# Numerators of an attention unit in groups of 7, 7 and 6 tiles, with a new order of all work

## The chip, the core and the metric

The kernel runs on one core of a Trainium2 chip. The core has a matrix engine (TensorE, PE in the profile, with its weight loads as PEld), a vector engine (VectorE, DVE), a scalar engine (ScalarE, ACT), a general engine (GpSimd, POOL) and a sync engine (SP) that here only issues transfers. The engines run side by side, each in the order of its own instructions, and wait for each other through semaphores. The matrix engine writes to PSUM, which has 8 banks of 2 KB in each of 128 partitions. The metric is the device time of one execution in microseconds (us), lower is better.

## The reference

Eight batches with eight heads of 576 tokens and 64 values each go through a linear attention with the feature map exp(p - max|p|), exp(-p - max|p|), where p is a projection to 128 features. The result, 4608 tokens of 512 values, goes through a feed-forward layer that takes the greatest of three products.

```
def phi(x):
    proj = x @ w_phi                                  # 64 -> 128
    proj = proj - max(|proj|, axis=-1)
    return concat([exp(proj), exp(-proj)], axis=-1)   # 256 features
kv  = phi(k)^T v ;  z = sum over tokens of phi(k)
num = phi(q) kv  ;  den = phi(q) z + 1e-6
x   = (num / den)       # heads side by side: (B*S, H*D)
h   = max(x @ w1, x @ w2, x @ w3)                     # 512 -> 768
out = h @ w_out                                       # 768 -> 512
```

## The kernel before, in words

The attention runs in 16 units of four heads (half a batch). The four heads are two pairs `pr`, each of two heads `ab`. The 576 tokens of a pair are kept in nine tiles of 64 tokens for each of its two heads, so a unit has 18 tiles of 128 rows; features stand on 128 partitions.

A unit goes through these pieces, each of them a `Node` of some kind. `L` and `Lv` load q, k and v in fp32 over SP's queue; `C` casts q and k to bf16 on POOL. From unit 4 on, `T` is one transposing transfer on SP's queue (line 495) that makes `qkT`, 18 tiles of 128x128; in the first four units TensorE transposes. `G` (line 518) projects q and k for up to four tiles into two banks; `r` (line 537) reduces them to their greatest absolute values on DVE, and `ek` (line 531) takes the exponentials of k on ACT. `R`, `mT` and `V` turn the maxima of q and write them as one row into `qkT` by a small transfer (line 553). `M` (line 597) projects q once more with the features on partitions, and `eq` (line 610) takes its exponentials, in five parts, one for each pair and head and one for the rest. `E`, `va` and `vd` scale v by the maxima of k. `K` (line 626) makes kv and z for both heads `ab` in two banks, and `kv` copies them out.

`N` (line 644) makes the numerators with the denominators beside them: a tile is 128 tokens by 65 values, two accumulating products. Before the change a group is one pair and one head `ab`: five tiles, the fifth of them from the rest. It needs the kv of its own `ab`, two `eq` of its part and the two of the rest. `x` (lines 650 and 651) takes the reciprocals of the five denominators and multiplies 128x320 values by them into `x_sb`, which is kept as pair, tile, head, value, so that a write steps over the other head. A unit has four such groups, each with a bank of its own. `X` (line 674) then carries all of `x_sb` to `xT` by one transposing transfer on SP's queue (the first two units use TensorE).

The feed-forward layer works on `xT` in nine chunks of 512 tokens, one for each batch and a ninth for the last 64 tokens of all batches. In a chunk there are twelve `up` and `up2` products of four matmuls each (line 697), whose results DVE and ACT take out, and four output tiles: four matmuls (line 725) and six (line 730), a copy `osb` (line 738) and a `store` (line 745). A tile of chunks 0 to 7 is stored by two transfers of 64 rows, one of chunk 8 by one transfer of 128 rows. The weights enter as differences, `wd` (line 768).

The order of all this comes from a planner and is written out: `PLAN` (lines 95 to 231) is a list of words such as `301S2@59.7`, which is node number 301, engine SP, buffer 2, due time 59.7. A letter T, D, A, G or S tells the engine (PE, DVE, ACT, POOL, SP). The kernel records the instructions in the list's order, engine by engine; nothing in the program waits for a due time. The due times also tell `fill` where TensorE's order has a gap in which it puts products on constant data (`idler`, line 827), nearly all before 28 us. The number of a node is its place in the order of creation, so the numbers differ between the two lists.

Three places of the list before, with the transposing transfer of a unit and the first projection that uses it:

```
301S2@59.7  ... 307T013201@67.2      unit 4
691S1@117.9 ... 712T107610@127.4     unit 10
756S0@146.2 ... 767T016110@154.6     unit 11
```

The functions that the change touches follow; the profile's line numbers stand beside them.

Of the kernel before, what the change touches and what calls it, by code (L numbers as in the profile page):

```python
# [19 lines left out]
P = 128  # L20
# [15 lines left out]
KPE = 1.04  # L36
GROUPS = [(0, 4), (4, 4), (9, 4), (13, 4), (8, 2)]
# [58 lines left out]
2D1@0.7 4A@0.7 85G1@0.7 10S1@0.7 3D@1.1 6S0@1.1 86G@1.5 8S@1.5 13S@2.0 0G@2.3 15S3@2.4 1076G@2.9 5D@3.4 159G0@3.6 12D2@3.9  # L96
158G@4.5 1079G@5.2 7A@5.7 1G@6.0 16T5@6.4 1077G@6.5 17D2@7.2 9A@7.4 27T103510@7.9 361S0@8.2 22T27@8.2 30D@8.4 31D@9.0 14A@9.1
26D@9.6 29A@9.7 20T4@9.9 18T6@10.0 21D@10.3 24A@10.3 25D@10.5 28A@10.8 19D@11.1 23A@11.3 42T54@11.4 46D@11.8 32T76@11.9 45D@12.1
43A@12.2 36D@12.4 44A@12.6 47A0@12.8 37T34@13.0 35D@13.0 39A@13.5 40D@13.6 93T7@13.8 33A@13.9 94D0@14.2 87D1@14.5 34A@14.5
115T012701@14.6 88S@14.7 58T30@14.7 118D@15.0 117A@15.0 61T5@15.3 41D@15.3 59A@15.5 64T2@15.8 48D1@15.9 38A@16.0 89T6@16.3  # L100
63A@16.5 67T4@16.9 60A@17.0 90D@17.1 91T0@17.2 66A@17.5 119D@17.7 51A@17.9 92D@18.1 62A@18.2 53G@18.3 1086T3@18.3 68A@18.6
65A@18.9 105T15@19.0 1087D1@19.0 69A@19.4 54G@19.4 55T2@19.5 228G1@19.7 108D@20.2 57A@20.3 227G@20.5 116A@20.7 95T14@20.9
56A@21.0 100T63@21.1 364G2@21.3 103D@21.6 102A@21.6 96A@22.1 98D@22.2 110T60@22.3 52G@22.4 97A@22.7 109D@22.8 166T2@23.1
162T1@23.2 113D@23.4 107A@23.5 11G@23.5 1078G@23.7 114D@24.0 106A@24.1 137T61@24.1 49G@24.5 101A@24.6 163D2@24.6 164T7@24.6
139A@25.0 167D@25.2 165D@25.5 1088T2@25.6 138A@25.6 50G@25.6 1090T1@26.0 124A1@26.1 1089D@26.3 112A@26.3 127G0@26.5 140T5@26.5
70T167@26.7 125G@26.7 1091A@26.8 99D@27.4 111A@27.7 126G@27.9 1096T2@27.9 72D@28.2 141A@28.2 71A@28.5 104D@28.5 142A@28.7
120A@29.3 173T106010@29.3 1097A@29.6 122G@29.6 183T51@29.6 1094T7@29.9 176D@29.9 174A@30.1 187D@30.5 186D@31.1 184A@31.2
73T31@31.3 75T4@31.6 175A@31.7 160D3@31.7 74D1@31.8 128T5@31.9 161S@31.9 1082G@32.1 1095A@32.1 134T6@32.4 362S1@32.4 76D0@32.4
185A@32.6 297S0@32.8 79T2@32.8 135A@33.1 178T47@33.2 80D0@33.4 131T3@33.5 136A@33.7 426S0@33.8 177D@34.0 77T2@34.2 121G@34.2
133A@34.3 1098T6@34.5 181D@34.6 129A@34.8 229D2@35.2 132A@35.3 78D1@35.3 123G@35.3 1080G@35.6 168T01@35.8 182D@35.9 1099A@36.0  # L110
143T032@36.1 171D@36.5 130A@36.5 179A@37.0 172D@37.1 188T60@37.3 231T5@37.4 144A@37.5 192D@37.7 145A@37.8 170A@38.1 191D@38.1
148T20@38.2 232D0@38.4 1092T4@38.5 196A1@38.5 190A@38.7 198G1@38.9 169A@39.0 149D1@39.0 189A@39.5 152T6@39.8 1093A@40.1
83T0@40.1 153D1@40.4 235T5@40.4 180A@40.6 146T4@40.7 197G@41.0 236D@41.0 84A@41.0 81T6@41.1 147D0@41.3 193T5@41.5 150T7@41.5
199A@41.7 233T1@41.8 82A@41.8 194D1@42.0 151D0@42.2 195S@42.3 154T4@42.4 234D@42.8 242T012601@42.8 230S@43.0 365G@43.1 155A@43.1
# [165 lines left out]
def kernel(  # L280
# [133 lines left out]
    def attention(u):  # L414
# [214 lines left out]
        for ab in range(2):  # L629
# [229 lines left out]
```

## Time and profile before

| what | value |
|---|---|
| median of 3 runs | 289.76 us (289.59 to 290.92) |
| the profiled execution | 290.44 us, its span 288.7 us |
| busy: PE, DVE, ACT, POOL | 279.6, 204.9, 197.8, 121.8 us |
| transfers | 51.45 MB, mean 178 GB/s |
| transposing transfers on SP | 12 of `qkT`, 14 of `xT` |

The span is the time from the first to the last instruction that the profiler saw on this core; the time of the execution has 1.7 us around it. A row of a view by line gives the place in the kernel, the engine, the operation with its tiles, the count, then the busy time in us and the mean of one in ns, and after the second bar the idle time of that engine just before, with what ended it. In a row of waits stand the engine and line that waited, what for, and then total, times and longest in us. [...]

### The profile page before, as it was taken

How to read it: one execution, taken by the hardware profiler on the slowest of the kernel's cores; microseconds unless marked ns; L12 is line 12 of the kernel's file. 1: busy time of each engine (PE TensorE's matmuls, PEld its weight loads, DVE VectorE, ACT ScalarE, POOL GpSimd, SP SyncE). 2: the span in 40 equal slices, each digit the busy share in tenths (PEclk: the TensorE clock that was granted, in tenths of full speed). 3: DMA queues.
4: the chain of work that ended last, by engine and by line, in shares of the span. 5: the costliest groups of instructions: out<-in, count | busy, mean ns of one | idle time of the engine just before them, and what ended most of it. 6: DMA issues, size and time to landing. Idle time of an engine off the chain costs nothing.

```text
span 288.7 us, 8634 instructions
## 1 busy us (share of the span) xinstructions
PE 279.6 (97%) x3587; PEld 155.0 (54%) x3587; DVE 204.9 (71%) x431; ACT 197.8 (69%) x456; POOL 121.8 (42%) x104
## 2 busy tenths in 40 slices
PE   8999999998999999999998999999999999999994
PEld 3466675465565655556455466565544654444452
DVE  3978888897999787967788778897976362156210
ACT  2799898998989998886896978977664501330021
POOL 8048969949517159564552634062162000000000
PEclk9999999999999999999999999999999999999999
DMA  7999979999989999999999988869400037610064
GB/s 184 275 251 209 236 280 205 283 309 210 178 208 257 254 262 238 246 213 272 209 231 226 257 177 201 210 136 143 82 4 0 2 75 144 139 30 0 6 157 130
DMA packets 68193, 51.45 MB, mean 178 GB/s; under 512 B 48762, under 2 KB 52922, under 8 KB 68154
## 3 DMA queue, kind: packets, MB, share of 16 engines
q1 hardware_dynamic: 63759, 45.55, 66.6%
q0 software_dynamic: 4000, 4.92, 9.9%
q8 instruction: 28, 0.46, 0.7%
q10 hardware_dynamic: 395, 0.43, 0.4%
q14 instruction: 11, 0.09, 0.1%
HBM read 34.64 MB, written 9.44 MB: 153 GB/s over the span
## 4 chain that ended last, share of the span: by engine, by line
PE 75%; DMA 15%; ACT 5%; DVE 2%; SPq 1%; issue 1%; ACTq 0%
PE ups L697 29%; PE ops L730 13%; DMA qkT<-qk_bf 9%; PE ops L725 9%; PE psn L644 5%; PE psq L518 5%; PE kvps L626 4%; PE psm L597 4%; DMA k_raw<-in_k_dram 2%; ACT Eq L610 2%; DMA xT<-x_sb 2%; PE pm L796 2%; ACT Ek L531 2%; DMA qkT<-mT 1%; DVE mqp L537 1%; PE idler L827 1%
## 5 line engine op out<-in xcount | busy, mean ns | idle before, releaser
L697 PE MATMUL ups<-xT,w_bf 128*128 128x512 bf16 x432 | 102.0, 379 | 0.2
L610 ACT ACTIVATE Eq<-psm 128x512 bf16<-128x512 f32 (+1 forms) x160 | 80.4, 575 | 18.6 <-PE psm L597 17.6
L531 ACT ACTIVATE Ek<-psk 128x512 bf16<-128x512 f32 (+1 forms) x160 | 81.8, 574 | 9.8 <-PE psk L518 7.3
L572 POOL TENSOR_TENSOR vab<-v_raw,em 128x1152 bf16<-128x1152 f32 (+1 forms) x35 | 67.2, 1929 | 50.2 <-ACT em L568 44.5
L697 PEld LDWEIGHTS <-w_bf 128*128 128x128 bf16 x432 | 40.2, 98 | 44.7 <-issue 0.4
L537 DVE TENSOR_REDUCE mqp<-psq 128x4 bf16<-128x512 f32 (+1 forms) x80 | 49.0, 633 | 10.8 <-PE psk L518 7.8
L537 DVE TENSOR_REDUCE mk<-psk 128x4 f32<-128x512 f32 (+1 forms) x80 | 49.4, 630 | 4.6 <-PE psk L518 2.7
L730 PE MATMUL ops<-wout_bf,hT 128*128 128x512 bf16 (+1 forms) x222 | 51.5, 373 | 0.0
L703 DVE TENSOR_TENSOR hT<-hT,ups 128x512 bf16<-128x512 bf16 x54 | 35.8, 682 | 11.9 <-PE ups L697 10.0
L738 ACT COPY osb<-ops 128x512 f32<-128x512 f32 (+1 forms) x21 | 12.2, 586 | 30.8 <-PE ops L730 13.4
L651 DVE TENSOR_TENSOR x_sb<-psn,rden 128x320 bf16<-128x320 f32 x64 | 31.5, 492 | 2.2
L644 PEld LDWEIGHTS <-Eq 128*128 128x128 bf16 x640 | 26.8, 97 | 11.4 <-DVE x_sb L651 0.4
L730 PEld LDWEIGHTS <-hT 128*128 128x128 bf16 x222 | 20.8, 98 | 21.2 <-DVE hT L703 0.2
L705 ACT ACTIVATE hT<-ups 128x512 bf16<-128x512 f32 x33 | 19.6, 607 | 18.1 <-PE ups L697 16.9
L644 PE MATMUL psn<-kv_sb,Eq 128*128 128x65 bf16 x640 | 29.3, 194 | 0.3 <-DVE x_sb L651 0.3
L738 DVE COPY osb<-ops 128x512 f32<-128x512 f32 (+1 forms) x16 | 10.7, 670 | 25.4 <-PE ops L730 12.7
L518 PE MATMUL psq<-w,qkT 64*128 64x128 bf16 x288 | 24.1, 217 | 2.7 <-DMA qkT<-qk_bf 2.6
L518 PEld LDWEIGHTS <-qkT 64*128 64x128 bf16 x576 | 16.5, 94 | 16.2 <-issue 9.6
L725 PE MATMUL ops<-xT 128*128 128x512 bf16 x96 | 24.5, 379 | 0.0
L518 PE MATMUL psk<-w,qkT 64*128 64x128 bf16 x288 | 24.1, 217 | 0.0
L466 POOL CAST qk_bf<-k_raw 128x1152 bf16<-128x1152 f32 x12 | 13.7, 1146 | 22.7 <-DMA k_raw<-in_k_dram 22.7
L597 PE MATMUL psm<-qkT,wphi_m 128*128 128x512 bf16 (+1 forms) x70 | 21.8, 358 | 0.3 <-DMA qkT<-mT 0.3
(71 smaller groups left out, 245.2 us busy)
## 6 DMA issues: line engine op xcount, KB each, us to landing
v_raw<-in_v_dram SPq DMA_DIRECT2D x16, 576.0 KB, 5.5
out_dram<-osb SPq DMA_DIRECT2D x65, 128.0 KB, 2.5
q_raw<-in_q_dram SPq DMA_DIRECT2D x12, 576.0 KB, 7.0
k_raw<-in_k_dram SPq DMA_DIRECT2D x12, 576.0 KB, 6.0
w_bf<-in_moe_w_dram POOLq DMA_DIRECT2D x3, 768.0 KB, 14.7
qk_bf<-in_q_dram POOLq DMA_DIRECT2D x3, 288.0 KB, 12.6
qk_bf<-in_k_dram POOLq DMA_DIRECT2D x3, 288.0 KB, 11.9
wout_bf<-in_moe_w_out_dram POOLq DMA_DIRECT2D x1, 768.0 KB, 20.9
```

The costliest lines, as they stand in the source:

```text
L518: nc.tensor.matmul(ps()[:, i, :], lhsT=cols[r, :], rhs=w2[r, c, :], start=True, stop=True)
L531: nc.scalar.activation(Ek[s]()[:, tiles_of(t0, n), :], of(1), EXP, scale=1.0 - 2.0 * s)
L537: nc.vector.tensor_reduce((mq, mk)[c]()[:, tiles_of(t0, n)], of(c), AXX, ALU.max, apply_absolute_value=True)
L572: (nc.vector if n_.eng == "DVE" else nc.gpsimd).tensor_tensor(vab()[:, g, t0:t1, 0:D], vb()[:, t0:t1, :], em()[:, g, t0:t1].unsqueeze(2).t ...
L597: nc.tensor.matmul(psm()[:, 0:w], lhsT=wphi_m, rhs=rhs, start=True, stop=True)
L610: nc.scalar.activation(Eqb()[s][:, cols], psm()[:, 0:w], EXP, scale=1.0 - 2.0 * s)
L644: nc.tensor.matmul(psn()[:, c, :], lhsT=Eqb()[g][:, t0:t0 + P], rhs=kv()[:, pr, ab, g, :], start=(g == 0), stop=(g == 1))
L651: nc.vector.tensor_tensor(x_sb()[:, pr, :, ab, :], psn()[:, :, 0:D], rden().to_broadcast([P, 5, D]), ALU.mult)
L697: nc.tensor.matmul(ups(), lhsT=w_bf[i + 1][:, ct, j * P:(j + 1) * P], rhs=tokens_of(ct), start=(ct == 0), stop=(ct == CT - 1))
L703: nc.vector.tensor_tensor(hT()[:, j, :], hT()[:, j, :], ups(), ALU.max)
L725: nc.tensor.matmul(ops_()[:, 0:width], lhsT=tile_of(ct, tt), rhs=line_w[c_i > MOVE][:, ct, cols], start=(ct == 0), stop=False)
L730: nc.tensor.matmul(ops_()[:, 0:width], lhsT=hT()[:, j, tt * P:(tt + 1) * P], rhs=wout_bf[:, j, cols], start=False, stop=(j == JT - 1))
```

## The change

The twenty tiles of a unit are numbered in one row: pair (0 or 1), then tile (0 to 4), then head `ab`. They are cut into groups of 7, 7 and 6. `x_sb` is kept as twenty tiles of 64 values, so that the values of a group lie side by side; the addresses of a value are the same as before. A group waits for the kv of both `ab`, for the `eq` of each part that its tiles touch, and for the two of the rest if it has a tile of it: the middle group waits for all ten. The reciprocals are 128x7 or 128x6, the products 128x448 or 128x384. The costs given to the planner for `N` and `x` are now by the tile.

With 32 nodes fewer (1442 for 1474) the whole list is new, planned with transposing transfers that take longer. The instructions of each engine stand in another order from start to end, and some pieces are on another engine: five output copies from ACT to DVE (ACT 21 to 16), seven `vd` from POOL to ACT (POOL 11 to 4), four `mT` from DVE to ACT, two of the six `wd` from POOL to DVE, and two of the first evacuations of `up` from DVE to ACT. There are 38 idlers for 43. SP issues as many loads, stores, T and X as before. The last output tile of the list is one of chunk 7, with two store transfers on SP; before it is one of chunk 8, with one on ACT. The three places of above, and the first `up` product of chunk 1 with the projection groups ahead of it, are in the new list:

```
293S2@58.1  ... 294T112100@66.4      unit 4
671S1@117.3 ... 692T006411@130.5     unit 10
734S0@147.1 ... 740T006711@155.8     unit 11
404T167@74.5 430T003111@75.9 389T2@76.1 435T50@76.6 1120T3@77.6
```

The core of the diff:

```
+NGROUPS = ((0, 7), (7, 14), (14, 20))
...
-        x_sb = buf("x_sb", 2, [P, 2, 5, 2, D], BF16)
+        x_sb = buf("x_sb", 2, [P, 20, D], BF16)
...
-        for pr in range(2):
-            for ab in range(2):
-                psn = bank("psn", [P, 5, W])
...
-                rden = buf("rden", 2, [P, 5, 1], FP32)
...
-                    nc.vector.reciprocal(rden(), psn()[:, :, D:W])
-                    nc.vector.tensor_tensor(x_sb()[:, pr, :, ab, :], psn()[:, :, 0:D], rden().to_broadcast([P, 5, D]),
-                                            ALU.mult)
-                first_eq = 4 * pr + 2 * ab
-                a = nd("N", {"PE": 0.32}, nmm, [n_kvs[ab]] + eqs[first_eq:first_eq + 2] + eqs[8:], [Eqb, kv, psn, x_sb])
-                divs[pr].append(nd("x", {"DVE": 0.62}, div, [a], [psn, x_sb, rden], locks=[psn]))
+        for n0, n1 in NGROUPS:
+            n, heads = n1 - n0, sorted({(i // 10, i % 2) for i in range(n0, n1)})
+            psn = bank("psn", [P, n, W])
+
+            def nmm(n0=n0, n1=n1, psn=psn):
+                for i in range(n0, n1):
+                    pr, c, ab = i // 10, i % 10 // 2, i % 2
+                    t0 = (8 * pr + 4 * ab + c if c < 4 else MT + pr) * P + (D if c == 4 and ab else 0)
+                    for g in range(2):
+                        nc.tensor.matmul(psn()[:, i - n0, :], lhsT=Eqb()[g][:, t0:t0 + P], rhs=kv()[:, pr, ab, g, :],
+                                         start=(g == 0), stop=(g == 1))
+
+            rden = buf("rden", 2, [P, 7, 1], FP32)
+
+            def div(n0=n0, n1=n1, n=n, psn=psn, rden=rden):
+                nc.vector.reciprocal(rden()[:, 0:n, :], psn()[:, :, D:W])
+                nc.vector.tensor_tensor(x_sb()[:, n0:n1, :], psn()[:, :, 0:D], rden()[:, 0:n, :].to_broadcast([P, n, D]), ALU.mult)
+            need = [e for pr, ab in heads for e in eqs[4 * pr + 2 * ab:4 * pr + 2 * ab + 2]]
+            if any(i % 10 // 2 == 4 for i in range(n0, n1)):
+                need += eqs[8:]
+            a = nd("N", {"PE": 0.0628 * n}, nmm, n_kvs + need, [Eqb, kv, psn, x_sb])
+            a = nd("x", {"DVE": 0.307 + 0.0666 * n}, div, [a], [psn, x_sb, rden], locks=[psn])
...
-            done.append(nd("X", {"SP": 1.5}, xdma, divs[0] + divs[1], [x_sb], pipe=1.9, hold=0.5, lat=1.5))
+            done.append(nd("X", {"SP": 1.5}, xdma, divs[0] + divs[1][1:], [x_sb], pipe=1.9, hold=0.5, lat=1.5))
```

More of the change, by code (lines that the diff above doesn't have):

```diff
@@ L100 @@
[L100 to L108, printed above, removed]
@@ new lines, in attention @@
+        for n0, n1 in NGROUPS:
[17 more added lines that the diff above has]
+            a = nd("x", {"DVE": 0.307 + 0.0666 * n}, div, [a], [psn, x_sb, rden], locks=[psn])
+            for j in range(2):
+                if any(i // 10 == j for i in range(n0, n1)):
+                    divs[j].append(a)
@@ L663, in tx @@
                     for c in range(5):
-                        nc.tensor.transpose(pxT()[:, c, :], x_sb()[:, pr, c, :, :].rearrange("p a d -> p (a d)"), ident)
+                        nc.tensor.transpose(pxT()[:, c, :], x_sb()[:, 10 * pr + 2 * c:10 * pr + 2 * c + 2, :].rearrange("p a d -> p (a d)"), ident)
                 def cx(n_, pr=pr, pxT=pxT):
@@ L675, in xdma @@
                     out=xT[:, b, ct0:ct0 + 2, :].rearrange("p q (t c) -> p (q t) c", c=P),
-                    in_=x_sb().rearrange("p q t a d -> p (q t a d)"))
-            done.append(nd("X", {"SP": 1.5}, xdma, divs[0] + divs[1], [x_sb], pipe=1.9, hold=0.5, lat=1.5))
+                    in_=x_sb().rearrange("p t d -> p (t d)"))
+            done.append(nd("X", {"SP": 1.5}, xdma, divs[0] + divs[1][1:], [x_sb], pipe=1.9, hold=0.5, lat=1.5))
         un["done"] = done
```

266 lines of the change are left out of this document (133 added, 133 removed).

## The prediction

> **What bounds the kernel now.** I read the page first, for the engine that is always busy and for the stretches where it is not, then the same by stage, then the waits of that engine, and last the chain.
>
> ```profile
> span 288.7 us, 8634 instructions
> PE 279.6 (97%) x3587; PEld 155.0 (54%) x3587; DVE 204.9 (71%) x431; ACT 197.8 (69%) x456; POOL 121.8 (42%) x104
> PE   8999999998999999999998999999999999999994
> PEclk9999999999999999999999999999999999999999
> ```
>
> TensorE is busy 279.6 of 288.7 us with a granted clock of nine tenths or more in all 40 slices. So the end moves only by what TensorE has to do, by where it stands idle, and by what follows its last product.
>
> ```profile
> 60.00:80.00 20.00, 18.94 (x329) 11.07 (x328) 16.90 (x38) 18.63 (x44) 12.95 (x11) 1.00 0.99 209
> 100.00:120.00 20.00, 19.67 (x301) 10.98 (x301) 17.24 (x38) 17.58 (x46) 15.36 (x11) 1.00 0.98 256
> 120.00:140.00 20.00, 19.57 (x296) 11.56 (x289) 15.40 (x36) 16.24 (x40) 7.47 (x5) 1.00 1.09 225
> 140.00:160.00 20.00, 18.79 (x249) 10.53 (x247) 16.23 (x33) 16.22 (x40) 10.46 (x8) 1.00 1.05 242
> 160.00:180.00 20.00, 20.00 (x311) 11.41 (x309) 14.95 (x33) 17.02 (x41) 9.49 (x8) 1.00 0.94 205
> ```
>
> The columns after the length are the busy time of PE, PEld, DVE, ACT and POOL, then clock, DMA share and GB/s. Beyond 60 us TensorE loses 1.06, 0.33, 0.43 and 1.21 us in four of these stages, 3.0 us together; in the fifth it loses nothing. Its waits for transfers over the whole run (total, times, longest):
>
> ```profile
> PE psq L518 <- DMA qkT<-qk_bf: 2.6, 3, 1.1
> PE psm L597 <- DMA qkT<-mT: 0.3, 1, 0.3
> PEld L518 <- DMA xT<-x_sb: 0.4, 1, 0.4
> ```
>
> They make 3.3 us, about what those stages lose, and each is for a transfer that SP issued. The chain of waits shows which (start, length from issue to landing):
>
> ```profile
> 58.29 9.42 DMA qkT<-qk_bf
> 104.52 4.02 DMA qkT<-mT
> 120.97 7.83 DMA qkT<-qk_bf
> 133.96 6.33 DMA xT<-x_sb
> 148.71 8.81 DMA qkT<-qk_bf
> ```
>
> By order on SP the three long ones are the transposing transfers T of units 4, 10 and 11. The list of before gave them, from issue to first projection, 7.5 us (`301S2@59.7` to `307T013201@67.2`), 9.5 (unit 10) and 8.4 (unit 11). They took 9.42, 7.83 and 8.81; unit 10's was issued 3.07 us after its due time. They landed at 67.71, 128.80 and 157.52, which is 0.5, 1.4 and 2.9 us behind the due time of their first use (67.2, 127.4, 154.6). So the lists can be read as an order with known spacing, and before lost its time against its own at these transfers. I take no duration from a list.
>
> **The change, part by part.**
>
> ```profile
> L651 DVE TENSOR_TENSOR x_sb<-psn,rden 128x320 bf16<-128x320 f32 x64 | 31.5, 492 | 2.2
> L644 PE MATMUL psn<-kv_sb,Eq 128*128 128x65 bf16 x640 | 29.3, 194 | 0.3 <-DVE x_sb L651 0.3
> L650 DVE RECIPROCAL rden<-psn 128x5 f32<-128x5 f32 x64 | 12.0, 187 | 8.5 <-PE psn L644 7.5 <-PE psq L518 0.5
> L738 DVE COPY osb<-ops 128x512 f32<-128x512 f32 x15 | 10.3, 687 | 21.1 <-DMA out_dram<-osb 12.6 <-PE ops L730 8.4
> L738 DVE COPY osb<-ops 128x256 f32<-128x256 f32 x1 | 0.4, 423 | 4.3 <-PE ops L730 4.3
> L572 DVE TENSOR_TENSOR vab<-v_raw,em 128x576 bf16<-128x576 f32 x1 | 0.7, 747 | 0.0
> L483 DVE COPY qkT<-tps 128x1024 bf16<-128x1024 bf16 x8 | 5.5, 682 | 2.2 <-PE tps L480 2.2
> L768 POOL TENSOR_TENSOR w_bf<-w_bf 128x1024 bf16<-128x1024 bf16 x6 | 12.7, 2124 | 0.0
> ```
>
> Groups of 7, 7, 6. The 640 numerator products stay: TensorE's work changes by nothing. On VectorE the two copies of 256 and 512 elements give (687-423)/256 = 1.03 ns an element from PSUM. A division of 5 tiles is 187+492 = 679 ns; of 7, 187+492+128x1.03 = 811; of 6, 745. A unit goes from 4x679 = 2716 to 2x811+745 = 2367 ns, 0.35 us less, 5.6 us over 16 units. VectorE is busy 71%, and TensorE waited 0.3 us in all for a division, so this saving is off the path: 0, and at most that 0.3. Against it a group now waits for both halves of kv and for up to seven tiles, and its bank is held 0.13 us longer; three banks instead of four are taken per unit. Covered by the other banks' work: 0 as well. x kept as twenty tiles has the same addresses, so transfer X is unchanged.
>
> Moves between engines. Output copies go from ACT to VectorE (21 to 16 on ACT), seven of the small `vd` copies from POOL to ACT, and two of the six weight differences from POOL, 2.12 us each, to VectorE. No row has that form there: 0.68 us (the 1024-element copy) to 1.22 (747 + 448x1.03 = 1208 ns, by the 576-element product). I take 1.2, nearest in form. They stand at due 44.2 and 49.5 with POOL's pieces due at 45.1 and 50.4; the engines' sums stay below TensorE's: 0, and if that cover fails at most 2.4.
>
> [...]
>
> The order of transfers. SP issues the same 14 X, 12 T and 13 small row transfers V, as many loads and stores. New spacings from T to first use: unit 4 8.3 us, 5 7.8, 10 13.2, 11 8.7, 12 7.7, the others 8.6 to 15.7. What a T needs, by its tile and by SP's timeline:
>
> ```profile
> L495 SPq DMA_TRANSPOSE qkT<-qk_bf x12: 2691/4322/6212, 43.9 to 184.9; - x12
> DMA to landing us min/median/max: 5.0/6.3/7.5
> ```
>
> ```profile
> 55.09 0.91 SPq L460 DMA_DIRECT2D q_raw<-in_q_dram  x2
> 57.82 0.37 SPq L460 DMA_DIRECT2D k_raw<-in_k_dram  x1
> 58.29 5.91 SPq L495 DMA_TRANSPOSE qkT<-qk_bf  x1
> 148.16 0.45 SPq L460 DMA_DIRECT2D v_raw<-in_v_dram  x1
> 148.71 5.46 SPq L495 DMA_TRANSPOSE qkT<-qk_bf  x1
> ```
>
> The issue alone takes 2.7 to 6.2 us, and the long ones stand directly behind loads: 0.47 us after a load for unit 4, 0.55 us for unit 11. In the new order the loads ahead of unit 4's T are due 2.7 us before it (54.9, 55.4 against 58.1), and unit 11's T has two stores ahead, due 4.5 us before it. So the 3.3 us of waits shown go, except a remainder between 1.1 (9.42 against 8.3 once more) and 0 (landing by 7.5). I take 0.5, nearer to the second, since the load directly ahead is gone. V of unit 8 has 3.0 us, against 4.02 before when a load stood directly ahead; now the last load is due 7 us earlier. X of unit 7 has 6.1 against 6.33, again without its load. 0 for both, at most 1.0 and 0.2.
>
> [...]
>
> What the longer spacing costs. In the new list the first `up` product of chunk 1 stands behind two projection groups of unit 6 (`430T003111@75.9`, `435T50@76.6`, `1120T3@77.6`), with little TensorE work between the first group and the reduction that frees the product's bank. So TensorE stands idle there for a VectorE piece. Bounds of all such places: 0, as its work is the same and it may run ahead of the list, and 1.9, the shift of the last product (due 280.2 to 282.1). I take 1.5: ACT is busy 18.63 of 20 us in that stage, so there is little running ahead.
>
> The tail.
>
> ```profile
> 278.52 5.05 SPq L745 DMA_DIRECT2D out_dram<-osb  x6
> 284.74 0.59 ACT L738 COPY osb<-ops 128x512 f32<-128x512 f32 x1 [0.92 <-PE ops L730]
> 285.35 0.34 ACTq L745 DMA_DIRECT2D out_dram<-osb  x1
> ```
>
> Before ends with a tile of chunk 8: one store, issued by ACT in 0.34 us. Now a tile of chunk 7 is last, with two stores on SP. Six such issues pass in 5.05 us, 0.84 each at the most; 0.45 (the load's issue above) is the least. Two take 0.9 to 1.7 us in place of 0.34; I take 1.1, so +0.8 (from +0.6 to +1.4).
>
> The first 45 us keep their pieces; five fill-in products fewer (38 for 43) stood in waits anyway: 0.
>
> **The sum.** The profiled execution took 290.44 us (span 288.7 and 1.7 around it), 0.68 above the median of 289.76. 290.44 - 3.3 + 0.5 + 1.5 + 0.8 = 289.94; less the same 0.68, 289.3 us at the median: no change that a measurement of this kernel tells (about 0.5%, 1.45 us).
>
> **The rivals.** First, faster: the spacing costs nothing, because the transfers land well before their use and TensorE runs ahead. 289.76 - 3.3 + 0.8 = 287.3. For it: median landing 6.3 against spacings of 7.7 and more. Against: ACT's 18.63 of 20.
>
> Second, slower: the late transfers move. The queue's filling decides, not the list: T of unit 4 behind its loads again and the T of units 5 or 12, with the smallest spacings (7.8, 7.7), late by 1.1 each. It decides from a landing above 8.3 us; 9.42 and 8.81 have been seen. Three such waits put the 3.3 back: 289.76 + 1.5 + 0.8 = 292.1; two 291.0. Against it: unit 5's and 12's T have few loads directly ahead.
>
> Third, also slower: ScalarE becomes the bound.
>
> ```profile
> L582 ACT CAST vab<-em 128x36 bf16<-128x36 f32 x7 | 2.6, 366 | 0.0
> L549 ACT COPY mT<-pmT 18x128 bf16<-18x128 bf16 x6 | 1.5, 249 | 0.5 <-PE pmT L545 0.5
> L705 ACT ACTIVATE hT<-ups 128x512 bf16<-128x512 f32 x33 | 19.6, 607 | 18.1 <-PE ups L697 16.9 <-DVE x_sb L651 1.0
> L738 ACT COPY osb<-ops 128x512 f32<-128x512 f32 x20 | 11.8, 596 | 28.3 <-DMA out_dram<-osb 11.9 <-PE ops L730 11.0 <-issue 5.3
> ```
>
> It takes seven `vd` copies (7x0.366), four `mT` (4x0.249) and two first evacuations (2x0.607) and gives five output copies away (5x0.596): +1.8 us. If all lies on the path, 289.3 + 1.8 = 291.1. Against it: its busy time is at most 18.63 of 20 us in the stages shown.
>
> Fourth: nothing tells; waits and spacing both stay half, 289.8.
>
> **Chances.** Forecast 0.45 (its own range 288.2 to 290.8), faster rival 0.22, moved waits 0.22, ScalarE 0.05, fourth 0.06. Faster by over 0.5% (below 288.3): the first rival and 0.02 of the forecast's edge, 0.24. Slower (above 291.2): 0.17 of the second, whose two-wait form stays inside the bound, and 0.02 each of the third and the forecast's edge, 0.21. Same 0.55. The range goes from the faster rival's 287.3 to 291.8, between the two-wait and the three-wait form of the slower one.
>
> **What would show it.** Right: projection lines with under 1 us of waits for qkT transfers where 2.6 stand now; TensorE idle for an engine, not for a transfer, near 75 us; reciprocals x48, products of 128x448 near 0.63 and 128x384 near 0.56 us; a last store of two issues on SP. Wrong: three T waits again, with loads directly ahead (second rival); a chain through ACT beyond its 5% share (third); TensorE at 20.00 in the stages at 60 and 140 us and no idle at 75 (first).

## The result: slower by 0.8%

| | median | runs |
|---|---|---|
| before, in the same comparison | 290.23 us | 288.89 to 291.99 |
| after | 292.21 us | 291.56 to 293.76 |
| ratio | 1.0077 | interval 1.0053 to 1.0102 |

The prediction was 289.3 us, with a range up to 291.8; the time lies above it. As a change it was 0.5 us down from the 289.76 measured until then; the comparison shows 2.0 us up from 290.23. Ratios leave out the slow executions, which medians and ranges include. The profiled execution of after took 293.76 us, 1.55 above its own median. Its page, with the same lines as shown of before and the shares of the chain:

```profile
span 292.0 us, 8575 instructions
PE 280.3 (96%) x3582; PEld 154.9 (53%) x3582; DVE 204.1 (70%) x399; ACT 200.3 (69%) x464; POOL 117.4 (40%) x98
PE   8998988999999998999999999999999999999993
PEclk9999999999999999999999999999999999999998
PE 85%; DMA 7%; ACT 5%; issue 1%; DVE 0%; SPq 0%
```

TensorE's busy time rose by 0.7 us and the span by 3.3: the larger part is idle time and tail. By stages of 20 us, first two rows of before that were not shown yet, then after (columns as before: length, then PE, PEld, DVE, ACT, POOL, clock, DMA share, GB/s):

```profile
20.00:40.00 20.00, 19.58 (x412) 13.00 (x408) 16.26 (x37) 18.50 (x44) 15.93 (x17) 1.00 1.15 258
40.00:60.00 20.00, 19.98 (x277) 11.58 (x275) 18.18 (x36) 18.00 (x42) 19.85 (x13) 1.00 0.91 246
```

```profile
20.00:40.00 20.00, 18.66 (x402) 12.55 (x401) 18.19 (x39) 17.74 (x44) 14.38 (x12) 1.00 1.15 260
40.00:60.00 20.00, 17.93 (x240) 10.19 (x239) 16.50 (x32) 16.97 (x39) 15.27 (x13) 1.00 0.76 229
60.00:80.00 20.00, 20.00 (x355) 12.08 (x354) 17.69 (x37) 18.79 (x46) 11.96 (x11) 1.00 1.12 210
80.00:100.00 20.00, 19.64 (x301) 10.87 (x300) 17.54 (x35) 18.48 (x43) 11.28 (x7) 1.00 1.00 238
100.00:120.00 20.00, 19.05 (x271) 11.04 (x269) 15.40 (x32) 18.01 (x46) 10.16 (x6) 1.00 0.90 248
140.00:160.00 20.00, 20.00 (x256) 10.89 (x255) 16.87 (x33) 16.49 (x39) 10.01 (x10) 1.00 0.88 247
```

The stages at 60 and 140 us, where before lost 1.06 and 1.21 us to transposing transfers, are full now. The new loss stands earlier, between 40 and 60 us: 2.05 us more, in a stage that the prediction had passed over. The 0.92 us less between 20 and 40 us are no loss of work. There TensorE's products on constant data (`idler`) alone take, before and then after:

```profile
20.00:40.00 20.00, 2.61 (x8) 1.00 1.15 258
```

```profile
20.00:40.00 20.00, 1.55 (x5) 1.00 1.15 260
```

So all other products take 16.97 us in before and 17.11 in after, and idle time stands where fill-in products stood. Later 0.36 and 0.62 us more are lost at 80 and 100 us. TensorE's waits in after, for products (PE) and for their weight loads (PEld):

```profile
PE psm L596 <- DMA qkT<-mT: 1.6, 3, 0.8
PE psn L644 <- issue: 1.3, 1, 1.3
PE kvps L625 <- issue: 0.7, 1, 0.7
PE tps L479 <- ACT qk_bf L441: 0.4, 1, 0.4
PEld L517 <- DMA qkT<-qk_bf: 0.4, 1, 0.4
```

The products' waits for transposing transfers, 2.6 us in before, are gone. Of the weight loads' waits for them, 3.3 us in before, 0.4 are left:

```profile
PEld L518 <- DMA qkT<-qk_bf: 3.3, 3, 1.6
```

The waits for the small row transfers V rose from 0.3 to 1.6 us (0.4, 0.8 and 0.5 for units 4, 8 and 9). And there are two stops, 1.3 us in the numerators of unit 1 at 40.0 and 0.7 in the kv products of unit 2 at 45.5, whose releaser is "issue": nothing that the profile shows was waited for. The tail in after (timeline):

```profile
286.32 0.81 PE L734 MATMUL ops<-wout_bf,hT 128*128 128x512 bf16 x3
286.65 2.25 SPq L749 DMA_DIRECT2D out_dram<-osb  x3
287.17 0.59 ACT L742 COPY osb<-ops 128x512 f32<-128x512 f32 x1 [1.61 <-PE ops L734]
```

From TensorE's last product (287.13) to the end (291.98) it takes 4.85 us; in before it was 284.70 to 288.66, 3.96.

Around the two stops, in stretches of 2 us, before and then after:

```profile
40.00:42.00 2.00, 2.00 (x50) 1.72 (x47) 1.89 (x8) 2.00 (x5) 2.00 (x2) 1.00 0.64 243
44.00:46.00 2.00, 2.00 (x58) 1.31 (x51) 2.00 (x5) 1.26 (x4) 2.00 (x2) 1.00 0.78 250
```

```profile
38.00:40.00 2.00, 2.00 (x44) 1.53 (x43) 1.75 (x5) 1.46 (x6) 1.41 (x1) 1.00 1.05 397
40.00:42.00 2.00, 0.71 (x20) 0.70 (x19) 0.68 (x3) 1.54 (x4) 2.00 (x2) 1.00 1.04 398
42.00:44.00 2.00, 1.99 (x48) 1.56 (x46) 1.86 (x5) 1.16 (x2) 0.78 (x1) 1.00 1.01 375
44.00:46.00 2.00, 1.48 (x73) 1.21 (x68) 2.00 (x4) 1.82 (x5) 0.38 (x2) 1.00 0.32 124
```

At the first stop the DMA engines are full (share 1.04, 398 GB/s). In the page's list of DMA queues (packets, MB, share) the second of these lines matters here:

```profile
q1 hardware_dynamic: 63759, 45.42, 65.4%
q8 instruction: 28, 0.46, 0.6%
```

The 28 packets on q8 are 16,384 bytes each. The trace has 7179 instructions of TensorE, 3582 products, as many weight loads and 15 that stand between, and 28 times 256 is 7168. Counted in program order, the two stops stand at instructions 1218 and 1474, which are 256 apart. From these numbers the author estimated that a packet holds 256 of TensorE's instructions, 64 bytes each (16,384/256), and that TensorE stopped for want of the next one; no row shows what a packet holds. For each packet one can give its lag: from TensorE's passing of one such border to the start of the packet that by this count belongs to the next. In after the two lags are 3.6 and 2.7 us, in before 1.7 and 1.0. After's two packets started at 39.04 and 43.98 us, and TensorE went on 2.2 and 2.3 us later. In all the traces of this document 17 stops of 0.5 us or more stand between 34 and 50 us; each is at one of these two borders, and each ended 2.2 to 2.6 us after the start of its packet. Most borders lie 5 to 15 us apart, and such lags cost nothing there (3.1 us at 27.1 in both kernels, 4.1 at 44.2 in before). In this stretch of short products 256 instructions last 4.3 us (35.57 to 39.89 and 39.89 to 44.21 in before), which less the 2.2 to 2.6 us leaves about 2 us of lag free, by estimate.

### The profile page after: what moved, and what is told of

Read it like the earlier page. It is cut to its first block, busy times and chain, and to the rows that moved or that the text cites. A ratio compares the mean times of both kernels' runs of the same rounds, so it can differ in the third digit from the quotient of the medians.

```text
span 292.0 us, 8575 instructions
## 1 busy us (share of the span) xinstructions
PE 280.3 (96%) x3582; PEld 154.9 (53%) x3582; DVE 204.1 (70%) x399; ACT 200.3 (69%) x464; POOL 117.4 (40%) x98
## 4 chain that ended last, share of the span: by engine, by line
PE 85%; DMA 7%; ACT 5%; issue 1%; DVE 0%; SPq 0%
PE ups L701 32%; PE ops L734 14%; PE ops L729 10%; PE psn L644 6%; PE kvps L625 6%; PE psq L517 5%; PE psm L596 5%; DMA qkT<-mT 4%; DMA k_raw<-in_k_dram 2%; ACT Ek L530 2%; ACT Eq L609 2%; PE pm L800 2%; PE tps L479 1%; PE psk L517 1%; PE idler L831 1%
## 5 line engine op out<-in xcount | busy, mean ns | idle before, releaser
L609 ACT ACTIVATE Eq<-psm 128x512 bf16<-128x512 f32 (+1 forms) x160 | 81.3, 571 | 17.0 <-PE psm L596 15.2
L742 DVE COPY osb<-ops 128x512 f32<-128x512 f32 (+1 forms) x21 | 14.0, 676 | 30.7 <-PE ops L734 26.0
L709 ACT ACTIVATE hT<-ups 128x512 bf16<-128x512 f32 x35 | 21.0, 610 | 19.3 <-PE ups L701 19.1
L651 DVE TENSOR_TENSOR x_sb<-psn,rden 128x448 bf16<-128x448 f32 (+1 forms) x48 | 28.9, 602 | 1.8 <-DVE rden L650 0.2
L644 PEld LDWEIGHTS <-Eq 128*128 128x128 bf16 x640 | 24.5, 98 | 7.5 <-issue 1.4
L742 ACT COPY osb<-ops 128x512 f32<-128x512 f32 (+1 forms) x16 | 9.2, 574 | 27.9 <-PE ops L734 22.8
L644 PE MATMUL psn<-kv_sb,Eq 128*128 128x65 bf16 x640 | 26.4, 194 | 1.3 <-issue 1.3
L517 PE MATMUL psq<-w,qkT 64*128 64x128 bf16 x288 | 25.1, 218 | 0.2
L625 PE MATMUL kvps<-vab,Ek 64*128 64x65 bf16 x1152 | 20.4, 190 | 0.7 <-issue 0.7
```

Source lines behind the costliest of these rows:

```text
L517: nc.tensor.matmul(ps()[:, i, :], lhsT=cols[r, :], rhs=w2[r, c, :], start=True, stop=True)
L609: nc.scalar.activation(Eqb()[s][:, cols], psm()[:, 0:w], EXP, scale=1.0 - 2.0 * s)
L625: nc.tensor.matmul(kvps[ab]()[:, t // NT, g, :], lhsT=Ek[g]()[r, t, :], rhs=vab()[r, g, t, :], start=(t + g == 0), stop=(t == UT - 1 and g ...
L644: nc.tensor.matmul(psn()[:, i - n0, :], lhsT=Eqb()[g][:, t0:t0 + P], rhs=kv()[:, pr, ab, g, :], start=(g == 0), stop=(g == 1))
```

## The experiments

The list orders the work of each engine; a due time does not hold an instruction back. A load moved in the list moves behind or ahead of other transfers of SP, and goes out when the queue comes to it (at 3.07 us for a list time of 8.2 in the run `l5_back`). Runs were compared with before on the same chip in several groups; each ratio is against before within its own group. In the diffs of a list only the words that differ are shown.

**A second execution of the changed kernel, unaltered.**

> The changed kernel once more, unaltered, for a second trace. Theory one (TensorE's instructions are refilled by transfers that queue with the loads, and five loads issued between 31 and 33 us make two refills late): it stops again inside the numerators of unit 1 near 40 us and inside K of unit 2 near 45 us, for nothing the profile shows, 1 to 2 us together, since the loads stand at the same place. Rival (a chance event of the one profiled execution, which at 293.76 us was 1.5 above the median of its kernel): no stop over 0.4 us there, and a span of 290.4 us or less. In both the waits for the row transfers of units 8 and 9 are there again (0.4 to 0.8 us each), and the end follows TensorE's last product by 4.9 us.

It took 291.76 us. Its lags were 1.9 and 1.9 us and there was no stop at 40 and 45 us. Instead it waited 1.4 us near 10 us for a cast and 1.4 near 119 for GpSimd. The stops depend on the execution: the DMA engines were as full here (share 1.02 to 1.07 from 36 to 44 us). And the slowness does not depend on the stops alone.

**One load fewer in the stretch: unit 4's raw V.**

```diff
-290S2@35.1
+290S2@65.4
```

> The load of v of unit 4 is moved on SP from the fifth of five loads at due 35.1 to due 65.4, ahead of the transposing transfer of unit 6; nothing else is altered. Theory one: the stops near 40 and 45 us shrink from 2.0 us to under 0.7, TensorE is busy over 19.0 us in the stage 40 to 60 where it was 17.9, and the kernel takes 0.7 to 1.5 us less than the changed kernel, 290.7 to 291.5 beside 292.2 and 290.2. Rival (the stops come from the pieces' own order, not from loads): both stops stay within 0.3 us and the time stays at 292.2.

293.17 us, ratio 1.0092 (1.0056 to 1.0128). In its trace, of an execution that took 295.64 us, the stops were 1.4 and 1.8 us, and the moved load now stood ahead of a transfer X, for which TensorE waited 1.4 us at 81.5. That this load alone is the cause is refuted.

**The same load in the order of before.** Unit 4's raw V goes early, and unit 6's takes its late place.

```diff
-428S0@55.0
+428S2@64.7
-298S2@64.7
+298S0@34.2
```

> The kernel before, with the loads of v of units 4 and 6 exchanged on SP: unit 4's goes from due 64.7 to 34.2, the fifth of five loads there, unit 6's from 55.0 to 64.7. Theory one: the kernel before, which had no stop over 0.4 us between 25 and 50 us, gets one or two, 0.7 to 2 us together, near 40 to 46 us for nothing the profile shows; in return the transposing transfer of unit 4 has a load less ahead and its wait falls from 1.1 us to under 0.6; time between 290.0 and 292.0 beside 290.2. Rival: no stop, and with the shorter wait 0.3 to 0.6 us faster than before.

288.85 us (288.41 to 289.43), ratio 0.9942 (0.9918 to 0.9965): faster than before. The stage at 60 to 80 us, 18.94 in before, reads

```profile
60.00:80.00 20.00, 19.79 (x334) 11.65 (x335) 17.89 (x42) 19.55 (x46) 13.31 (x10) 1.00 1.00 190
```

The stops that were expected did not come: four loads now stood behind unit 2's raw V, as many as in the changed kernel, and the lags were 2.4 and 2.2 us.

**The tail.** The last product of chunk 7 with its copy and store goes ahead of chunk 8's last ones.

```diff
-1387T@282.1  1388A0@283.6  1389S@284.4
+1387T@278.5  1388A0@280.0  1389S@280.8
```

> In the changed kernel the last tile of chunk 7 is moved ahead of the two last pieces of chunk 8, so that a tile of chunk 8 with one store is last, as in the kernel before; the rest is the same. Theory one (the two stores at the end cost what the sum said): the time from TensorE's last product to the end goes from 4.9 us to 4.0 to 4.2, and the kernel is 0.7 to 0.9 us faster than the changed kernel, 291.3 to 291.5. Rival (the last transfer's landing sets the end, whichever tile it is, and the store of 256 KB lands later than one of 128 KB): below 0.3 us gained.

292.30 us, ratio 1.0068 (1.0043 to 1.0094). In its trace the tail is 4.10 us in place of 4.85, so the 0.75 is there; but this trace had stops of 1.4 and 1.6 us and the time does not tell it from the changed kernel.

**The groups alone.** The new groups and the twenty tiles of x, with the list of before; each unit's three groups stand in three of its four old places.

```diff
+NGROUPS = ((0, 7), (7, 14), (14, 20))
...
-        x_sb = buf("x_sb", 2, [P, 2, 5, 2, D], BF16)
+        x_sb = buf("x_sb", 2, [P, 20, D], BF16)
```

> One part alone: numerators in groups of 7, 7 and 6 and x as twenty tiles, in the order of before (three of a unit's four old places carry the three new groups, the loads and turns stay where they were). Theory one (the order costs the time, the groups nothing): 290.2 us, ratio to before 0.998 to 1.002; the 48 products of VectorE show 16 x 0.35 us less busy time and the span does not; the turn of unit 4 is waited for as in before, about 1 us near 66 us; no stop over 0.4 us for nothing that the profile shows between 35 and 50 us. Rival (the groups cost it: the longer group holds its PSUM bank and VectorE longer): ratio 1.004 or more, with waits of TensorE for VectorE behind the numerators.

290.78 us, ratio 1.0013 (0.9994 to 1.0031). VectorE's busy time is 201.3 us in place of 204.9. Unit 4's turn is waited for as in before, and there is no stop near 40 or 45 us:

```profile
PE psq L518 <- DMA qkT<-qk_bf: 1.5, 1, 1.5
```

The groups cost nothing that this measures; the rest of the change, the new order with its pieces on other engines, does.

**The groups with the two loads exchanged.** The exchange above, on top of the groups alone.

```diff
-416S0@55  290S2@64.7
+416S2@64.7  290S0@34.2
```

> As the run of the groups alone, with the two loads exchanged that made the order of before faster (the load that stood ahead of unit 4's turn is issued at 34 us, another one in its place at 64.7). If the groups cost nothing and the exchange is worth what it was in the order of before (0.58%), ratio 0.992 to 0.997, 288.2 to 289.3 us. If the groups cost time, 0.998 or more. The new order's start, loads and row transfers are not in it, so no stop over 0.5 us between 35 and 50 us and none for rows.

291.06 us, ratio 1.0026 (1.0002 to 1.0050). Unit 4's turn was issued for 5.85 us and landed 9.39 after its issue, against 4.54 and 6.55 in the exchange alone, and TensorE waited 1.3 us for it. The exchange brought nothing here; what makes this transfer long in one and short in the other was not found.

**The load at 2.4 us back at 8.2.**

```diff
-351S0@2.4
+351S0@8.2
```

> The changed kernel with one load moved back: that of unit 5's raw rows, issued at 2.4 us behind unit 0's, goes to 8.2 us, where the order of before has it. Theory (this load takes bandwidth from the small loads at the start): TensorE's first wait for a cast near 10 us, 0.45 to 1.4 us in three traces of the new order, falls under 0.4 us; the time falls by 0.4 to 1.0 us, ratio 1.003 to 1.006. Rival (the start does not set the end, or the wait has another cause): the wait stays, or the time stays at 292.2 us, ratio 1.007.

292.28 us, ratio 1.0069 (1.0043 to 1.0095). The load went out at 3.07 us in place of 2.59: it had nothing to wait for, so the list only put it behind unit 0's raw V (in before it went out at 8.01). The wait near 10 us was gone from this trace, and stops of 1.4 and 1.3 us stood at 40 and 45. For the time it is inconclusive: what the start gained is not seen in it.

**The last load of weights back at 23.7 us.**

```diff
-1046G@20.9
+1046G@23.7
```

> The changed kernel with one load of weights on POOL's queue issued where the order of before has it, at 23.7 us instead of 20.9. Theory (the loads that flow at 35 to 45 us come later and tighter in the new order because of this load, and hold up the 16,384-byte packets of the instruction queue): the two stops near 40 and 45 us, together 2.0 to 3.2 us in three of four traces of the new order, fall under 0.5 us, the packets start within 2.4 us of TensorE's crossing of a block; ratio 1.001 to 1.004. Rival (chance, or the rest of the new order): stops of 1 us or more stay; ratio 1.006 to 1.009.

292.12 us, ratio 1.0069 (1.0046 to 1.0091). The load was issued at 23.04 us in place of 20.99; stops of 1.3 and 1.0 us, lags 3.6 and 2.6. It is not this load's place.

**Three of the five loads later, and the reverse in before.** In the changed kernel (`loads_off`):

```diff
-288S1@33.0  290S2@35.1  414S0@40.6
+288S1@43.5  290S2@50.7  414S0@46.6
```

> The changed kernel with three of the five loads between 31 and 41 us issued later: the first half of unit 4's raw rows at 43.5 us (33.0), unit 4's raw V at 50.7 (35.1), unit 6's rows at 46.6 (40.6). Theory (the packets that refill TensorE's instructions start late because these loads keep the DMA engines full until 44 us): the engines empty before 41 us, the stops near 40 and 45 us, together 2.0 to 3.2 us in five of six traces of the new order, fall under 0.6 us, and the time falls by 1.2 to 2.4 us to ratio 0.999 to 1.004. Rival (the small products of this stretch, not the loads, or another trait of the order): stops of 1 us or more stay, ratio 1.006 to 1.009. Rival (a moved load delays a turn): no stops, but a wait of 0.5 us or more for a turn at 50 to 70 us, ratio 1.004 to 1.008.

In before, with the exchange (`loads_on`), five loads into the same stretch:

```diff
-362S1@32.4  297S0@32.8  426S0@33.8  296S1@43.5  298S2@64.7  428S0@55.0
+362S1@31.7  297S0@32.1  296S1@33.0  298S0@35.1  426S0@36.0  428S2@64.7
```

> The kernel before with the five loads of the new order put into the same stretch: 31.7, 32.1, 33.0, 35.1 and 36.0 us (in before three at 32.4 to 33.8, one at 43.5, and unit 4's raw V at 64.7, where unit 6's stands now). Theory (these loads make the instruction packets late): the engines are full until about 44 us as in the changed kernel, and stops for nothing that the profile shows appear near 40 and 45 us, 1 us or more together, which none of four traces of this order had above 0.4; the time stands 0.5 to 1.2% above that of the order with the exchange alone. Rival (the loads do not do it): no stop over 0.5 us there, time within 0.3% of the exchange alone.

In `loads_on` one of the five, unit 5's second half, moved ahead of unit 2's raw V and went out at 24.87 us, so four loads stand in the stretch, at 33.09 to 34.63 us. The first gave 291.48 us, ratio 1.0046 (1.0024 to 1.0069). The second gave 291.33 us, ratio 1.0030 (1.0002 to 1.0058). The stops, first with the loads later, then with them put into before (waits between 34 and 50 us):

```profile
PE psn L644 <- issue: 1.4, 1, 1.4
PE kvps L625 <- issue: 0.2, 1, 0.2
```

```profile
PE kvps L626 <- issue: 0.9, 1, 0.9
PE pxT L664 <- issue: 0.7, 1, 0.7
```

The second stop shrinks from 0.7 to 0.2 us with the loads that were taken away (lag 2.1), and both stops come with the loads that were put in (2.7 and 3.0), in an order that showed none above 0.3 us in five other traces. The first stop stayed; two loads still stood ahead of it.

**The exchange a second time.**

> The kernel before with the two loads exchanged, a second time and with more runs, because the same exchange in the kernel with the groups alone brought nothing (ratio 1.0026). If the exchange is worth what it was, ratio 0.992 to 0.996 and no wait for unit 4's turn near 66 us; if the first result was chance, ratio 0.998 to 1.002 and that wait is back at about 1 us, with the turn landing over 9 us after its issue.

289.72 us (288.47 to 292.47), ratio 0.9975 (0.9945 to 1.0004), run beside the last two. The stage from 60 to 80 us has 19.79 us of work again, so the wait for unit 4's turn is gone both times; in this trace two other waits stand elsewhere:

```profile
PE psm L597 <- DMA qkT<-mT: 1.9, 1, 1.9
PE psq L518 <- DMA qkT<-qk_bf: 1.2, 2, 1.0
```

So the exchange is worth 0.6% once and 0.25% the second time. The loads of `loads_on` take the exchanged order from 0.9975 to 1.0030, in one comparison whose intervals just touch.

**Three mends at once.** The three loads later, the load at 2.4 us back and the tail.

> The changed kernel with all three mends at once: the three loads later, the load at 2.4 us moved to 8.2, and the last product of chunk 7 brought forward from 282.1 to 278.5 us. If the stops (2.0 to 3.2 us), the wait at 10 us (0.4 to 1.4) and the longer tail (0.75) each count in full, 288.0 to 289.5 us, ratio 0.993 to 0.997, faster than both kernels. If only the tail and the start do, 0.999 to 1.003; if none does, 1.006 or more.

291.38 us, ratio 1.0032 (1.0005 to 1.0058), with stops of 1.4 and 0.5 us: less was gained than the sum of the three, and the first stop is still there.

**All five loads later.**

```diff
-352S1@31.7  289S0@32.1  288S1@33.0  290S2@35.1  414S0@40.6
+352S1@38.0  289S0@42.0  288S1@41.0  290S2@50.7  414S0@46.6
```

> The changed kernel with all five loads between 31 and 41 us issued later: 31.7 to 38.0, 32.1 to 42.0, 33.0 to 41.0, 35.1 to 50.7 and 40.6 to 46.6 us. With three of them moved, the stop near 45 us went and that near 40 stayed (1.4 us; its packet started 3.6 us after TensorE's crossing of the block). Theory (the two loads at 31.7 and 32.1 make this packet late as the others made the next): lag under 2.5 us, stops near 40 and 45 us together under 0.6 us, time 0.3 to 0.6% below that with three loads moved, ratio 0.999 to 1.002. Rival (the first stop has another cause, such as the load of weights that fills the engines until 34 us): lag of 3.5 us and 1.4 us of stop stay, ratio 1.004 to 1.007. Rival (the later loads delay unit 5's casts or turn): a wait of 0.5 us or more at 45 to 70 us.

290.58 us, ratio 1.0013 (0.9982 to 1.0044), no stop, lags 1.0 and 0.4. But in its trace the granted clock was 0.73, 0.50 and 0.92 between 22 and 28 us, which put TensorE 1.5 us behind. The same kernel was traced once more, at a clock of 1.00:

> The run with the five loads later, a second look, because in the first TensorE's clock was granted 0.50 to 0.92 between 22 and 28 us, which put it 1.5 us behind and past the loads. If the later loads removed the stops, none of over 0.5 us near 40 and 45 us at full clock; if the lower clock did, 1 us or more together, as in the run with the three mends and the five loads (1.0 and 1.6 us).

Lags 1.8 and 0.8, no stop; 291.48 us, with a wait of 1.0 us at the start and one of 1.3 for a transfer X. So the lower clock is not needed for it. That it was the loads rests on all the runs together, since one trace of the changed kernel with its own loads had no stop either.

**The five loads with the other two mends.**

```diff
-351S0@2.4  1387T@282.1  1388A0@283.6  1389S@284.4
+351S0@8.2  1387T@278.5  1388A0@280.0  1389S@280.8
```

> As the run with the five loads later, with the load at 2.4 us at 8.2 and chunk 7's last product at 278.5 us as well. If the stops, the start and the tail each count, 0.2 to 0.4% below the five loads alone, ratio 0.995 to 0.999: this would put the changed kernel level with or below before. If only the loads count, the ratio of the five loads alone.

290.57 us, ratio 1.0007 (0.9973 to 1.0041). Its trace had stops of 1.0 and 1.6 us with lags of 3.4 and 3.4, in an execution of 291.71 us, 1.1 above the median; one trace does not tell how often a kernel stops. TensorE passed the first border at 34.7 us, against 36.8 and 36.0 in the two traces without stops, with the weights and the first load still under way; that this is the reason was only argued.

**Every load behind unit 2's row transfer.** The first of the five had kept its place in SP's queue. Now it is moved behind.

```diff
-352S1@38.0
+352S1@40.0
```

> As the run with the five loads later, but the first of them (unit 5's second half) goes behind unit 2's row transfer: its list time of 38.0 had left it in its place in SP's queue, and it was issued at 31 to 33 us all the same. Only the raw V of unit 2 is then left ahead of the row transfer. Theory (the packet that TensorE waits for near 40 us is late because loads share the DMA engines with the last load of weights until 38 us): lag of the packet under 2.5 us, stops near 40 and 45 us together under 0.6 us at full clock, ratio 0.997 to 1.001. Rival (this packet is late behind the load of weights alone): 1 us or more of stop stays near 40 us, ratio 1.001 to 1.004.

290.93 us, ratio 1.0010 (0.9981 to 1.0039), lags 1.0 and 0.4, no stop. SP's issues, first in the changed kernel, then here:

```profile
30.84 0.37 SPq L459 DMA_DIRECT2D v_raw<-in_v_dram  x1
31.39 0.88 SPq L459 DMA_DIRECT2D k_raw<-in_k_dram  x2
32.37 0.41 SPq L459 DMA_DIRECT2D q_raw<-in_q_dram  x1
32.88 0.41 SPq L459 DMA_DIRECT2D v_raw<-in_v_dram  x1
39.41 0.91 SPq L552 DMA_DIRECT2D qkT<-mT  x1
40.37 0.41 SPq L459 DMA_DIRECT2D q_raw<-in_q_dram  x1
```

```profile
30.89 0.37 SPq L459 DMA_DIRECT2D v_raw<-in_v_dram  x1
39.45 0.91 SPq L552 DMA_DIRECT2D qkT<-mT  x1
40.48 0.38 SPq L459 DMA_DIRECT2D k_raw<-in_k_dram  x1
```

In before (two loads stand directly behind the row transfer there too, but that goes out 2.4 us later):

```profile
31.25 0.37 SPq L460 DMA_DIRECT2D v_raw<-in_v_dram  x1
31.73 0.92 SPq L460 DMA_DIRECT2D k_raw<-in_k_dram  x2
32.70 0.46 SPq L460 DMA_DIRECT2D q_raw<-in_q_dram  x1
41.77 0.92 SPq L553 DMA_DIRECT2D qkT<-mT  x1
42.74 0.42 SPq L460 DMA_DIRECT2D v_raw<-in_v_dram  x1
```

The first two stretches of after that were shown above read in this run:

```profile
38.00:40.00 2.00, 2.00 (x48) 1.57 (x47) 1.75 (x5) 1.46 (x6) 1.42 (x2) 1.00 0.07 12
40.00:42.00 2.00, 2.00 (x54) 1.82 (x50) 1.73 (x5) 2.00 (x5) 2.00 (x2) 1.00 0.38 39
```

The DMA share falls from 1.05 to 0.07 and TensorE has no idle time in these 4 us.

**These loads and the tail.**

```diff
-1387T@282.1  1388A0@283.6  1389S@284.4
+1387T@278.5  1388A0@280.0  1389S@280.8
```

> The changed kernel with the loads of the run before (unit 2's row transfer ahead of them) and the last product of chunk 7 brought forward to 278.5 us, the start left as it is. If the loads' 0.6% and the tail's 0.75 us add, 289.9 us beside a before of 290.5, ratio 0.996 to 1.000: the changed kernel level with or just below before, no stop over 0.5 us near 40 and 45 us, and 4.1 us from the last product to the end. If the tail moves only the trace's end and not the time, or the stops come back as they did with the three mends and five loads, 1.001 to 1.004.

290.01 us, ratio 0.9985 (0.9958 to 1.0012). No stop, lags 1.2 and 0.2, and 4.11 us from the last product to the end. In this trace too the granted clock was 0.62 and 0.52 from 22 to 26 us; the run before it had no stop at a clock of 1.00.

All traces together, at these two borders, worked out from the packets' starts and TensorE's weight loads:

| order and loads | traces | lags, us | stops near 40 and 45, us |
|---|---|---|---|
| before's order (before, groups, both exchanges, groups with exchange) | 5 | 1.3 to 2.4 and 0.5 to 2.2 | none above 0.3 |
| before's order with the loads of `loads_on` | 1 | 2.7 and 3.0 | 0.7 and 0.9 |
| new order, its loads (after, again, tail, start, weights) | 5 | 3.6 to 3.7 and 2.6 to 3.3; again 1.9 and 1.9 | 1.3 to 1.4 and 0.7 to 1.6; again none |
| one load fewer | 1 | 3.7 and 3.8 | 1.4 and 1.8 |
| three loads later (alone, with mends) | 2 | 3.6 to 3.7 and 2.1 to 2.3 | 1.4 and 0.2 to 0.5 |
| five loads later (two executions; with mends) | 3 | 1.0 to 1.8 and 0.4 to 0.8; with mends 3.4 and 3.4 | none; with mends 1.0 and 1.6 |
| all behind the row transfer (alone, with tail) | 2 | 1.0 to 1.2 and 0.2 to 0.4 | none |

A lag up to 2.4 us cost at most 0.5 us; from 2.6 on, every one cost 0.7 or more. The number of loads ahead does not give the first lag in these traces: four in the exchanged order of before go with 1.4 (with the new groups), 1.9 and 2.4 us, four in the changed kernel with 3.6 and once 1.9, one (five loads later) with 1.0, 1.8 and 3.4. Only with none, in two traces, is it 1.0 and 1.2.

## Why the prediction was wrong, step by step

**The first 45 us.** "The first 45 us keep their pieces; five fill-in products fewer (38 for 43) stood in waits anyway: 0." On the fill-in products this was right. As the price of these 45 us the 0 failed, and it is the largest miss. The pieces of the engines stay, but SP has four loads instead of three behind unit 2's raw V, and a fifth behind a row transfer that goes out 2.4 us earlier than in before, and the DMA engines are full until 44 us (share 1.01 from 42 to 44 us in after, 0.20 in before). In after two packets of q8 started 3.6 and 2.7 us behind their borders, in a stretch where 256 of TensorE's instructions last only 4.3 us in before. Moving the loads behind the row transfer takes the ratio from 1.0077 to 1.0010, 0.67% or 1.9 us (the intervals, from 1.0053 and up to 1.0039, do not overlap), and the two stops make 2.0 us in the trace of after. Both signs were run: loads taken away and loads put into before. What stays open is which trait of the new list makes the first packet late: the exchanged order of before has the same four loads behind unit 2's raw V, and no stop. Behind the two borders near 35 and 40 us, lags were 0.2 to 1.2 us wherever the DMA share of the next 2 us was under 0.5 (five lags); with a share of 0.9 or more they lay anywhere from 1.3 to 3.8. How a load holds a packet up was not shown: no row here shows a single DMA engine.

**The waits for T.** Right: the products' 2.6 us are gone, and 0.4 of the weight loads' 3.3 are left. Unit 4's took 7.91 us with the nearest load issued 3 us ahead of it, against 8.3 us of room, and was not waited for, so the remainder of 0.5 did not come. But the prediction counted the other half of the transfers too low: V at 0, "at most 1.0"; it was waited for 1.6 us, 1.3 more than in before (units 4, 8 and 9; unit 9's landed 5.82 us after its issue). This wait is 0 to 1.9 us in the other traces, with no pattern that the runs explain.

**What the longer spacing costs.** Sized at 1.5 us; no wait shows it. TensorE stands in the stage at 60 to 80 us with 20.00 us of work, and there is no idle near 75. By the prediction's own signs this is its faster rival, whose 287.3 us did not come because of the losses elsewhere. The shift of 1.9 us in the list's last due time was no price that a wait shows. That the term was too high by 1.5 us hid part of the miss: without it the sum would have been 287.8.

**The tail.** Right: +0.8 taken, 4.85 less 3.96 is 0.89 measured. The last mend gives 0.75 of it back in the trace, and the ratio goes from 1.0010 to 0.9985, 0.7 us; the intervals overlap, so the time alone would not show it.

**Groups of 7, 7, 6.** Right: off the path, by the run of the groups alone (ratio 1.0013). The rows by form in after:

```profile
L651 DVE TENSOR_TENSOR x_sb<-psn,rden 128x448 bf16<-128x448 f32 x32 | 20.0, 624 | 1.1
L651 DVE TENSOR_TENSOR x_sb<-psn,rden 128x384 bf16<-128x384 f32 x16 | 8.9, 558 | 0.7 <-DVE rden L650 0.2
L772 DVE TENSOR_TENSOR w_bf<-w_bf 128x1024 bf16<-128x1024 bf16 x2 | 1.4, 682 | 0.0
```

The products take 624 and 558 ns where 0.63 and 0.56 us were forecast. A weight difference on VectorE takes 682 ns, the lower of the two bounds and not the 1.2 us that was taken. In after no piece of GpSimd runs beside the two differences (44.88 and 51.12 us): behind each the program lets GpSimd copy one of its elements, and GpSimd waited 4.7 us for these two copies. The prediction had not counted this wait; no wait of TensorE in after is for GpSimd.

**The rivals.** The second, "the late transfers move", came in part, as V and not as T. That its price for three such waits, 292.1 us, lies beside the measured 292.21 is chance: the largest loss has another cause. ScalarE is busy 200.3 us and is not the bound. The late packets were in no rival: they are on q8, and the kernel's list has no word for them.

**The account.** In ratios: changed kernel 1.0077; loads behind the row transfer 1.0010; tail as well 0.9985. What the prediction expected to gain, the 3.3 us of waits, is seen as full stages at 60 and 140 us but hardly in the time: with the loads and the tail mended the kernel is level with before. Where the rest of that gain goes is not settled. Part of it is in no row of waits: TensorE's busy time without the fill-in products (14.0 us in before, 12.9 in after) is 265.6 us in before and 267.4 in after, for the same 3544 products, and 267.1 to 267.9 in the five other traces of the new order with as many records. "TensorE's work changes by nothing" holds for the count and not for this time; what makes it longer was not found. Besides, the traces show single waits of 0.7 to 1.4 us in changing places: the first casts near 10 us, V, and transfers X.

Also open are why the lags were 1.9 us once with the changed kernel's own loads, and why the exchange of two loads failed with the new groups. The fastest version of these runs is the order of before with the exchange, 288.85 and 289.72 us, below both kernels; the second time its interval just includes 1.

## What to carry to other kernels

The page can list a queue of instruction packets beside those of the data; here it was q8, 28 packets of 16,384 bytes. Where an engine runs many short instructions while loads fill the DMA engines (here 256 in 4.3 us, and a share of 1.01 to 1.07), look at the packets of the instruction queue, and try putting loads that have time behind such a stretch; here that gave back 1.9 us. A load's place among the transfers of its queue counted here, not the time that the list gave it: one that had nothing to wait for went out as soon as the queue reached it (at 3.07 us for a list time of 8.2). When a planner gives a new order, compare the queues of transfers stage by stage over the whole run, also where no engine's work has changed.

## What was not expected of the hardware

In after the queue q8 moved 28 packets of 16,384 bytes, beside 7179 instructions of TensorE, and in all the traces every stop of 0.5 us or more between 34 and 50 us, 17 of them, stood at one of two places that are 256 instructions apart. That a packet holds 256 instructions is the author's estimate from these numbers. Behind the two borders near 35 and 40 us a packet started 0.2 to 1.2 us after the border where the DMA share of the next 2 us was under 0.5, and 1.3 to 3.8 us after it where the share was 0.9 or more. At the 17 stops TensorE went on 2.2 to 2.6 us after the start of the packet. Lags of 2.6 to 3.8 us came with stops of 0.7 to 1.8 us, which the profile files under "issue", in a stretch where 256 instructions last 4.3 us in before.
